# Counting TensorE's instruction records in the planner that orders an FNet + S4D kernel

## The chip, the cores and the metric

The kernel runs on one core of a Trainium2 chip. The core has a matrix engine (TensorE, in the profile PE, with its weight loads shown apart as PEld), a vector engine (VectorE, DVE), a scalar engine (ScalarE, ACT), GpSimd (POOL), and a queue engine (SyncE, SP) that issues nearly all transfers here. Each engine works through its own instructions in the order in which the program issued them, and waits on semaphores for the others.

The metric is the device time of one execution in microseconds, as the median of several runs. Before the change it is 602.95 us (three runs: 599.85, 602.95 and 603.13 us).

## What is computed

Two layers that share nothing but the output, whose halves are laid side by side:

```python
# A: FNet mixing of x[2048, 512]
a = einsum("sd,ed->se", x, dft_hid_re);  b = einsum("sd,ed->se", x, dft_hid_im)
y_a = einsum("ts,se->te", dft_seq_re, a) - einsum("ts,se->te", dft_seq_im, b)

# B: S4D convolution of u[2048, 512] with a kernel K of 512 x 2048, made from 128 modes
dt = exp(log_dt);  A = -exp(log_A_real) + 1j * A_imag;  C = (C_real + 1j * C_imag) * dt
P = exp((A * dt)[:, :, None] * arange(2048))
K = 2 * einsum("dn,dnl->dl", C, P).real
y_b = irfft(rfft(u, 4096) * rfft(K, 4096), 4096)[:2048] + u * D_skip

out = concatenate([y_a, y_b], axis=-1)
```

## The kernel before

**FNet** (class `Fnet`) is plain matrix work. Every fp32 operand is split into a rounded part `hi` and a rest `lo` (ScalarE copies at line 184, VectorE subtracts at line 188), and a product is three matmuls at line 304: hi·hi, hi·lo and lo·hi. There are 640 such steps of three matmuls, 128x128 by 128x512 each. An *item* is one streamed operand with four steps, one for each of four PSUM accumulators. Eight groups of 16 items make the sequence transform of x (results go out to DRAM as `p`), and four groups of 8 items multiply `p` with the hidden-dimension matrices. A split item lies in one of three pairs of buffers, a raw operand in one of four. Steps of FNet have the lowest priority (urgency 5): they are the filler between everything else.

**The S4D side** (class `Ssm`) is a chain. VectorE and ScalarE build tables `t1` and `t2` of the modes' powers for 16 chunks of 32 channels (`tables1`, `tables2`). For each chunk `taps` multiplies the tables on TensorE to get 32 channels of K. There is one `t2` buffer: `tables2` begins the next chunk's `t2` when the matmuls of `taps` have read the last one. Two chunks of K make one `stage1_k` (the first step of K's transform), whose result is stored as `xk`. `stage1_u` does the same for u, with u split in parts. For each of four quarters of the channels, four times, `product` takes the second step of both transforms (line 935), multiplies the spectra on VectorE, and takes a first inverse step (line 970), stored as `zs`. Two `inverse` calls per quarter (line 1015) end it and write `out_yb`. The last quarter of K is stored in four pieces (`store_k`), so that its products may begin one by one.

The S4D matmuls are small: a 32x32 or 64x32 tile against a few dozen to a few hundred columns. The change calls a group of them *dry*, because it uses up many instructions in little time. An fp32 matmul leaves two pairs of weight load and matmul records in the trace, so `taps` with its 64 matmuls is 256 records in about 2 us, where an FNet step of three matmuls is 6 records in about 0.7 us. If a first inverse step is waiting when `taps` is placed, the two are issued together (`other.run(got)`): 64 records at line 970 and then 256 at line 754. In the profile eight of the 16 `taps` are such joined groups.

**The order is planned, not written.** The program runs a small simulation (class `Plan`) while it emits instructions. Each piece of work is a Python generator that yields what it needs: an event, a buffer (`Sem`), or an engine with an estimated time, such as `yield "pe", 0.685` ahead of one FNet step or `yield "pe", 1.78 + (0.87 if other else 0)` ahead of `taps`. `run` keeps a list of pieces that ask for an engine and always takes the one with the smallest `key`: earliest possible start, then urgency, then age. Having taken it, it moves that engine's clock on by the estimate and resumes the generator, which issues its instructions then and there. So the order of `key` becomes the program order of every engine and of SP's queue. In the plan TensorE is only ever held up by data and buffers.

Of the kernel before, what the change touches and what calls it, by code (L numbers as in the profile page):

```python
# [48 lines left out]

HOP, RESULT, LATENCY = 0.3, 0.15, 3.3  # L50
STREAM = 5
APART = None, True


class Sem:


    def __init__(self, n):
        self.free, self.waiting = [0.0] * n, []
# [7 lines left out]
class Plan:  # L67
# [3 lines left out]
    def __init__(self):  # L71
        self.free, self.ready, self.now = {}, [], 0.0
        self.count, self.streaming = 0, True

    def spawn(self, gen, urgency=0, at=None):
        self.step([self.now if at is None else at, urgency, self.count, gen, None, None], None)
# [47 lines left out]

    def key(self, p):
        engine, _, *urgency = p[4]
        return max(p[0], self.free.get(engine, 0.0)), urgency[0]() if urgency and urgency[0] else p[1], p[2]

    def run(self):

        while self.ready:
            p = min(self.ready, key=self.key)
            engine, dur, *_ = p[4]
            start = self.key(p)[0]
            self.ready.remove(p)
            if engine == "pe":
                stream = p[1] >= STREAM
                if stream != self.streaming:
                    dur += 0.12 if stream else 0.1
                self.streaming = stream  # L140
            self.free[engine] = start + dur
            p[0] = start + dur + (LATENCY if engine.startswith("dma") else 0.0)
            self.step(p, start)
# [14 lines left out]
class Fnet:  # L158
# [38 lines left out]
    def warm(self):  # L197

        z, ps = self.pool.tile([128, DM], F32, name="y", bufs=STAGED), self.psum.tile([128, DM], F32, name="acc")
        yield "dve", 0.3  # L200
        self.nc.vector.memset(z, 0.0)
        yield "pe", 2.6
        for n in range(3):
            self.nc.tensor.matmul(ps[:, :256], z[:, :128], z[:, 256:], start=n == 0, stop=n == 2)

# [77 lines left out]
    def matmuls(self):  # L283
        nc = self.nc
        for g in self.groups:
            still = (self.x, self.x_ev) if g[0] == "s" else (self.w, self.w_ev)
            items, acc = self.items[g], []
            for batch in [[i] for i in items[:-BATCH]] + [items[-BATCH:]]:
                for d in range(4):
                    if batch[0][3] == 0:  # L290
                        yield self.acc
                        acc.append(self.psum.tile([128, DM], F32, name="acc"))
                    for i in batch:
                        k = i[3]
                        yield self.m_ev[i]
                        yield still[1][k] if k or d or g != self.groups[0] else self.x0_ev
                        (shi, slo), (mhi, mlo) = still[0][k], self.m[i]
                        yield "pe", 0.685
                        cols = slice(128 * d, 128 * d + 128)
                        three = (shi, mhi), (shi, mlo), (slo, mhi)  # L300
                        if still[1][k] is self.x_ev[0] and not d:
                            three = three[::2] + three[1:2]
                        for n, (l, r) in enumerate(three):
                            nc.tensor.matmul(acc[d], l[:, cols], r, start=k == 0 and n == 0,  # L304
                                             stop=k == len(items) - 1 and n == 2)
                        if d == 3:
                            self.plan.put(self.ss)
                            self.split_ahead -= 1
                            if i[:3] == ("s", 3, 1) and k < 8:
                                self.plan.set(self.x_free[k])  # L310
                    if batch[-1] is items[-1]:
                        self.plan.spawn(self.evacuate(g, d, acc[d]), -1)
# [53 lines left out]
class Ssm:  # L366
# [133 lines left out]
    def params(self, par, alpha, dt):  # L500

        v = self.nc.vector
        n = par.shape[2]
        yield "dve", dve(n), *APART
        v.tensor_tensor(par[:, 0], alpha, dt, op=OP.mult)
        yield "dve", dve(n), *APART
        v.scalar_tensor_tensor(par[:, 1], par[:, 1], 1.0 / (2 * math.pi), dt, op0=OP.mult, op1=OP.mult)
        yield "dve", dve(n), *APART
        v.tensor_tensor(par[:, 2], par[:, 2], dt, op=OP.mult)
        yield "dve", dve(n), *APART  # L510
        v.scalar_tensor_tensor(par[:, 3], par[:, 3], -1.0, dt, op0=OP.mult, op1=OP.mult)
# [224 lines left out]
    def taps(self, ks, n, done):  # L736

        nc = self.nc
        yield self.t1_ev[n]
        yield self.t2_ev[n]  # L740
        other = self.waiting.pop(0) if self.waiting else None
        got = yield from self.banks(2 if other else 1)
        k, p = got[0]
        yield "pe", 1.78 + (0.87 if other else 0)
        if other:
            other.run(got)
        t1, t2 = self.t1.pop(n), self.t2
        for o in range(2):
            ps = p[:, o, 256:].rearrange("p (i l) -> p i l", i=4)
            for i in range(4):  # L750
                for c in range(2):
                    for j in range(4):
                        d = 16 * o + 4 * i + j
                        nc.tensor.matmul(ps[32 * j:32 * j + 32, i], t1[:, d, c], t2[:, d, c],  # L754
                                         start=c == 0, stop=c == 1, tile_position=(0, 32 * j))
        self.plan.put(self.t1s)
        self.plan.put(self.t2s)
        self.taps_left -= 1
        if other:
            self.plan.set(other)  # L760
        while self.waiting and not self.taps_left:
            self.plan.set(self.waiting.pop(0))
        yield "act", act(512)
        nc.scalar.activation(ks[:, 8 * (n % 2):8 * (n % 2) + 8].rearrange("p (o i) l -> p o (i l)", o=2),
                             p[:, :, 256:], AF.Copy)
        if other:
            other.leave(k)
        else:
            self.give(k)
        done()  # L770

    def stage1_k(self, ks, n, ev):

        nc = self.nc
        yield ev
        yield "pool", 0.2
        nc.gpsimd.tensor_tensor(ks[:, :, 0], self.dskip[:, 16 * n:16 * n + 16], ks[:, :, 0], op=OP.add)
        yield self.const_ev
        got = yield from self.banks(2)
        yield "pe", 1.82  # L780
        for a in range(2):
            for j in range(4):
                r = slice(32 * j, 32 * j + 32)
                nc.tensor.matmul(got[j // 2][1][:, j % 2], self.f1k[r, a], ks[r, :, 32 * a:32 * a + 32],  # L784
                                 start=a == 0, stop=a == 1, tile_position=(32 * j, 0))
        self.plan.put(self.kss)
        yield self.xks
        xs = self.tab.tile([128, 32, 64], F32, name="xk_sb")
        for h, (k, p) in enumerate(got):
            for j in range(2):  # L790
                o = 32 * h + 16 * j
                yield from self.copy(xs[:, :, o:o + 16], p[:, j].rearrange("p (i l) -> p l i", i=16), n == 7 and j)
            self.give(k)
        xk = self.xk[n // 2].rearrange("s c l d -> (s c) l d")[:, :, 64 * (n % 2):64 * (n % 2) + 64]
        if n < 7:
            yield "dma", load(1024)
            for k in range(4):
                nc.sync.dma_start(xk[:, 8 * k:8 * k + 8], xs[:, 8 * k:8 * k + 8])
        else:
            for k in range(4):  # L800
                self.plan.spawn(self.store_k(xk, xs, k), 1)
            yield self.xk_ev[3][3]
        self.plan.put(self.xks)
        if n % 2 and n < 7:
            for ev in self.xk_ev[n // 2]:
                self.plan.set(ev)
        if n == 7:
            self.plan.set(self.tab_ev)
# [22 lines left out]
    def stage1_u(self, k, name):  # L831
        nc, b = self.nc, self.sets[0]
# [7 lines left out]
        yield "dve", dve(1024)  # L840
        nc.vector.tensor_tensor(lo, u, hi.bitcast(F32), op=OP.subtract)
        got = yield from self.banks(2)
        yield "pe", 1.42
        f_hi, f_lo = self.f1u_hi, self.f1u_lo
        for m in range(2):
            for n, (f, v) in enumerate(((f_hi, hi), (f_hi, lo), (f_lo, hi))):
# [6 lines left out]
        for m in range(2):  # L853
            n = 2 * k + m
# [69 lines left out]
    def product(self, b, h, q, got, done):  # L924
        nc, v, a = self.nc, self.nc.vector, self.nc.scalar
        uk = b.pool.tile([128, 2, 2, 2, 2, PART], F32, name="uk", bufs=b.n)
        yield "pe", 1.86
        xt = self.xt[h, q]
        for r in range(2):
            for c in range(2):  # L930
# [44 lines left out]
            yield w  # L975
        if w.got is None:
            got = yield from self.banks(2)
            yield "pe", 0.95
            w.run(got, False)
        self.plan.put(b.uks)  # L980
        yield b.zbs
# [22 lines left out]
    def inverse(self, b, h, i, n):  # L1004
# [4 lines left out]
        for o in range(0, n, 8):  # L1009
            nc.sync.dma_start(z[:, o:o + 8], self.zs[h].rearrange("s c l d -> (s c) l d")[:, n * i + o:n * i + o + 8])  # L1010
        (k, ps), = yield from self.banks(1)
        yield "pe", 0.1 + 0.1025 * n
        for w in range(n // 2):
            for y in range(2):
                nc.tensor.matmul(ps[64 * y:64 * y + 64, w // 4, PART * (w % 4):PART * (w % 4) + PART],  # L1015
# [87 lines left out]
```

## Time and profile before

| | us |
|---|---|
| median of the three runs | 602.95 |
| the profiled execution's own time | 596.78 |
| its span, first to last instruction | 595.0 |
| TensorE (PE) busy | 579.2 |
| VectorE (DVE) busy | 508.1 |
| ScalarE (ACT) busy | 387.1 |

The profiled execution is 6.2 us shorter than the median of the runs and 3.1 us shorter than the shortest of them. It ran at a granted TensorE clock of 0.999. A busy share is an average over the whole span; what matters is which wait ends last at each place. By fortieths of the span, VectorE is 80% busy or more in all slices but one from the second until about 490 us, where the tables are done, and far less busy in the rest. TensorE is 80% busy or more in all slices but the last.

### The profile page before, as it was taken

How to read it: one execution, taken by the hardware profiler on the slowest of the kernel's cores; microseconds unless marked ns; L12 is line 12 of the kernel's file. 1: busy time of each engine (PE TensorE's matmuls, PEld its weight loads, DVE VectorE, ACT ScalarE, POOL GpSimd, SP SyncE). 2: the span in 40 equal slices, each digit the busy share in tenths (PEclk: the TensorE clock that was granted, in tenths of full speed). 3: DMA queues.
4: the chain of work that ended last, by engine and by line, in shares of the span. 5: the costliest groups of instructions: out<-in, count | busy, mean ns of one | idle time of the engine just before them, and what ended most of it. 6: DMA issues, size and time to landing. Idle time of an engine off the chain costs nothing.

```text
span 595.0 us, 14993 instructions
## 1 busy us (share of the span) xinstructions
PE 579.2 (97%) x5990; PEld 442.6 (74%) x5990; DVE 508.1 (85%) x898; ACT 387.1 (65%) x748; POOL 4.8 (1%) x12
## 2 busy tenths in 40 slices
PE   8999999999999999999998989998999999989997
PEld 6877777778778777777876768776877777766786
DVE  7999999999999999999998969998999993265420
ACT  5789877976785777749683858594866454353432
POOL 0000000000000000000000000000000000000000
PEclk9999999999999999999999999999999999999999
DMA  8977847665483376636877485557697946997474
GB/s 278 385 259 263 286 153 278 234 218 192 124 271 96 102 202 200 163 106 190 222 230 230 156 217 153 140 165 216 223 292 216 293 139 189 269 335 238 139 255 143
DMA packets 141238, 125.84 MB, mean 211 GB/s; under 512 B 46192, under 2 KB 106352, under 8 KB 140912
## 3 DMA queue, kind: packets, MB, share of 16 engines
q1 hardware_dynamic: 140880, 124.48, 67.5%
q8 instruction: 47, 0.77, 0.5%
q10 hardware_dynamic: 288, 0.39, 0.2%
q14 instruction: 23, 0.19, 0.1%
HBM read 82.12 MB, written 42.73 MB: 210 GB/s over the span
## 4 chain that ended last, share of the span: by engine, by line
PE 85%; DVE 4%; ACT 3%; DMA 3%; issue 3%; SPq 1%; DVEq 0%; ACTq 0%
PE acc L304 65%; PE f L754 5%; PE f L935 4%; PE f L970 3%; PE f L784 3%; PE f L1015 2%; PE f L849 2%; DVE lo L188 1%; DMA p<-y 1%; DMA out_yb<-zl 1%; ACT hi L184 1%; DMA xt<-xk 1%; DMA cs<-in_ldt 1%; ACT y L327 1%; DVE x_lo L188 1%
## 5 line engine op out<-in xcount | busy, mean ns | idle before, releaser
L304 PE MATMUL acc<-hi,x_hi 128*128 128x512 f32 x640 | 258.1, 403 | 1.7 <-ACT y L327 1.5
L304 PE MATMUL acc<-lo,x_hi 128*128 128x512 f32 x640 | 250.3, 391 | 0.3 <-DVE lo L188 0.3
L304 PE MATMUL acc<-hi,x_lo 128*128 128x512 f32 x640 | 249.8, 390 | 0.0
L558 DVE TENSOR_TENSOR prod<-t,cs 128x1024 f32<-128x1024 f32 (+3 forms) x192 | 164.1, 870 | 9.9 <-ACT t L696 8.1
L304 PEld LDWEIGHTS acc<-hi,x_hi 128*128 128x128 f32 x640 | 120.2, 188 | 49.3 <-issue 19.8
L184 ACT ACTIVATE hi<-raw 128x512 fp32r<-128x512 f32 x160 | 100.5, 629 | 77.1 <-PE acc L304 61.0
L188 DVE TENSOR_TENSOR lo<-raw,hi 128x512 fp32r<-128x512 f32 x160 | 109.4, 686 | 41.1 <-ACT hi L184 39.7
L304 PEld LDWEIGHTS acc<-hi,x_lo 128*128 128x128 f32 x640 | 120.3, 188 | 26.4 <-DVE x_lo L188 0.3
L304 PEld LDWEIGHTS acc<-lo,x_hi 128*128 128x128 f32 x640 | 120.5, 188 | 23.9 <-DVE lo L188 1.2
L567 DVE TENSOR_TENSOR t<-prod 128x512 f32<-128x512 f32 (+4 forms) x192 | 94.4, 511 | 1.2
L574 ACT ACTIVATE square<-t 128x256 f32<-128x256 f32 (+1 forms) x64 | 36.6, 571 | 22.9 <-DVE t L567 22.7
L327 ACT ACTIVATE y<-acc 128x512 f32<-128x512 f32 x47 | 27.9, 595 | 17.1 <-PE acc L304 14.4
L754 PEld LDWEIGHTS f<-t,t 128*32 128x32 f32 x2048 | 29.7, 110 | 12.3 <-issue 7.7
L754 PE MATMUL f<-t,t 128*32 128x64 f32 x2048 | 32.7, 220 | 5.9 <-issue 5.4
L947 ACT ACTIVATE uk<-f 128x1024 f32<-128x1024 f32 x32 | 31.9, 1013 | 9.8 <-PE f L935 6.4
L935 PE MATMUL f<-xt,w 64*32 64x256 f32 x1024 | 31.5, 379 | 2.7 <-DMA xt<-xk 2.0
L950 DVE TENSOR_TENSOR z<-uk 128x512 f32<-128x512 f32 x32 | 21.9, 686 | 13.4 <-ACT uk L947 13.4
L935 PEld LDWEIGHTS f<-xt,w 64*32 64x32 f32 x1024 | 18.6, 106 | 13.7 <-issue 7.4
L439 ACT ACTIVATE z<-f 128x512 f32<-128x512 f32 x28 | 15.7, 597 | 18.2 <-PE f L970 10.1
L587 DVE TENSOR_TENSOR t<-square 128x128 f32<-128x128 f32 (+1 forms) x64 | 24.7, 385 | 0.0
L633 ACT ACTIVATE cs<-cs 128x352 f32<-128x352 f32 x32 | 15.9, 540 | 11.8 <-DVE cs L628 11.7
L581 DVE SCALAR_TENSOR_TENSOR t<-t 128x128 f32<-128x128 f32 (+2 forms) x48 | 22.3, 465 | 0.3
(89 smaller groups left out, 433.7 us busy)
## 6 DMA issues: line engine op xcount, KB each, us to landing
raw<-in_sT SPq DMA_DIRECT2D x127, 256.0 KB, 3.2
p<-y SPq DMA_DIRECT2D x32, 256.0 KB, 3.4
xk<-xk_sb SPq DMA_DIRECT2D x32, 256.0 KB, 4.0
xt<-xu SPq DMA_DIRECT2D x32, 256.0 KB, 3.9
xt<-xk SPq DMA_DIRECT2D x32, 256.0 KB, 5.0
zs<-z SPq DMA_DIRECT2D x32, 256.0 KB, 3.0
zl<-zs SPq DMA_DIRECT2D x16, 512.0 KB, 6.5
raw<-p SPq DMA_DIRECT2D x32, 256.0 KB, 3.4
```

What stands on the lines that cost most here:

```text
L184: self.nc.scalar.activation(hi, src, AF.Copy)
L188: self.nc.vector.tensor_tensor(lo, src, hi.bitcast(F32), op=OP.subtract)
L304: nc.tensor.matmul(acc[d], l[:, cols], r, start=k == 0 and n == 0, stop=k == len(items) - 1 and n == 2)
L327: self.nc.scalar.activation(y, ps, AF.Copy, scale=-1.0 if g[2] == 1 else 1.0)
L558: self.nc.vector.tensor_tensor(p.rearrange("p k d c m -> p k (d c) m"), src.rearrange("p d c l -> p (d c) l")[:, None, :, rows].to_broadca ...
L567: self.nc.vector.tensor_tensor(dst[:, :, :, rows], p[:, 0], p[:, 1, :, ::-1], op=OP.add)
L574: self.nc.scalar.activation(sq, t[:, :, :, m // 2:m], AF.Square)
L581: self.nc.vector.scalar_tensor_tensor(t[:, :, 1, m:2 * m:2], t[:, :, 0, m // 2:m], 2.0, t[:, :, 1, m // 2:m], op0=OP.mult, op1=OP.mult)
L587: self.nc.vector.tensor_tensor(t[:, :, 0, m:2 * m:2], box[0][:, :, 0], box[0][:, :, 1], op=OP.subtract)
L754: nc.tensor.matmul(ps[32 * j:32 * j + 32, i], t1[:, d, c], t2[:, d, c], start=c == 0, stop=c == 1, tile_position=(0, 32 * j))
L935: nc.tensor.matmul(both[:, :, c], self.w2[rows, 2 * q + r, xx, 32 * c:32 * c + 32], xt[rows, r, xx], start=True, stop=True, tile_position= ...
L947: a.activation(uk[:, r].rearrange("p g n c d -> p g (n c d)"), p, AF.Copy)
```

## The change

No arithmetic, buffer or transfer is added or removed. What changes is how `Plan` computes the start of a piece of work on TensorE, and so which of two pieces it takes.

- Each request for TensorE now carries the number of records that it will issue: 12 for the warm-up, 6 for an FNet step, 257 for `taps` alone, 322 for `taps` with a waiting inverse step, 33 for `stage1_k`, 25 for `stage1_u`, 130 for `product`, 65 for an inverse step alone, and `4 * n + 1` (65) for `inverse`.
- `Plan` counts the records issued (`done`) and keeps a list of instruction blocks of 256 records with the time at which each arrives. In its model, block k is asked for 3.0 us after record 256k + 129 and no sooner than 4.3 us after the one before, arrives 2.4 us after it was asked for, and is needed at record 256k + 449.
- `fetched` works out, for a request of n records, how long it would be held by a block that has not arrived, within the request or within as many records behind it. `key` adds this to the start.

A request with such a hold therefore counts as starting later, and any FNet step that is ready before then is taken first. In the diff `r[3]` is the number of records and `r[1]` the estimated time.

```diff
+BLOCK, ASKS, LASTS = 256, 129, 449
+ASKED, APART_BY, COMES = 3.0, 4.3, 2.4
...
         self.count, self.streaming = 0, True
+        self.done, self.blocks, self.asked = 0, [], -9.0
...
     def key(self, p):
         engine, _, *urgency = p[4]
-        return max(p[0], self.free.get(engine, 0.0)), urgency[0]() if urgency and urgency[0] else p[1], p[2]
+        start = max(p[0], self.free.get(engine, 0.0))
+        if engine == "pe":
+            start += self.fetched(p[4], start)[0]
+        return start, urgency[0]() if urgency and urgency[0] else p[1], p[2]
+
+    def fetched(self, r, start):
+
+
+        n, dur = r[3], r[1]
+        wait, blocks, asked = 0.0, list(self.blocks), self.asked
+        while BLOCK * len(blocks) + ASKS < self.done + n:
+            at = start + wait + dur * max(0, BLOCK * len(blocks) + ASKS - self.done) / n
+            asked = max(at + ASKED, asked + APART_BY)
+            blocks.append(asked + COMES)
+        for k, b in enumerate(blocks):
+            run = BLOCK * k + LASTS - self.done
+            if 0 <= run < n:
+                wait += max(0.0, b - (start + wait + dur * run / n))
+            elif 0 <= run < 2 * n:
+                wait += max(0.0, b - (start + wait + dur + 0.11 * (run - n)))
+        return wait, blocks, asked
...
             if engine == "pe":
+                _, self.blocks, self.asked = self.fetched(p[4], max(p[0], self.free.get(engine, 0.0)))
+                self.done += p[4][3]
...
-        yield "pe", 2.6
+        yield "pe", 2.6, None, 12
...
-                        yield "pe", 0.685
+                        yield "pe", 0.685, None, 6
...
-        yield "pe", 1.78 + (0.87 if other else 0)
+        yield "pe", 1.78 + (0.87 if other else 0), None, 322 if other else 257
...
-        yield "pe", 1.82
+        yield "pe", 1.82, None, 33
...
-        yield "pe", 1.42
+        yield "pe", 1.42, None, 25
...
-        yield "pe", 1.86
+        yield "pe", 1.86, None, 130
...
-            yield "pe", 0.95
+            yield "pe", 0.95, None, 65
...
-        yield "pe", 0.1 + 0.1025 * n
+        yield "pe", 0.1 + 0.1025 * n, None, 4 * n + 1
```

## The prediction

> **What bounds the kernel now.** I read the page first: the busy shares, the queues, and the costliest groups.
>
> ```profile
> span 595.0 us, 14993 instructions
> PE 579.2 (97%) x5990; PEld 442.6 (74%) x5990; DVE 508.1 (85%) x898; ACT 387.1 (65%) x748; POOL 4.8 (1%) x12
> q8 instruction: 47, 0.77, 0.5%
> PE 85%; DVE 4%; ACT 3%; DMA 3%; issue 3%; SPq 1%; DVEq 0%; ACTq 0%
> ```
>
> TensorE is busy for 579.2 of 595.0 us, so it is idle for 15.8 us, and no reordering can save more than that. It leaves 5990 + 5990 = 11980 records, and queue q8 brought 47 instruction packets of 0.77 MB together, 16 KB each: 255 records to a packet. So q8 carries TensorE's program, a packet for each 256 records. Next the waits of TensorE, then the chain of waits where it says "issue", and its end:
>
> ```profile
> PE f L754 <- issue: 5.4, 3, 2.1
> PE f L935 <- DMA xt<-xk: 2.0, 1, 2.0
> PE acc L304 <- ACT y L327: 1.5, 2, 0.9
> PE acc L304 <- DVE lo L188: 0.3, 1, 0.3
> ```
> ```profile
> 314.43 1.63 issue
> ...
> 349.83 2.09 issue
> ...
> 406.81 1.67 issue
> ...
> 580.27 1.90 PE f L1015 x32
> 582.17 9.08 PE acc L304 x39
> ```
>
> Columns of the chain are start, length, and what. A third of TensorE's idle time, 1.63 + 2.09 + 1.67 = 5.39 us, lies in three holes at line 754 (`taps`), in which no semaphore is waited for. The steps of FNet (line 304) wait only 1.8 us in all of 1920 matmuls: their operands are nearly always there. The chain ends in 9.08 us of FNet matmuls with nothing else, so the end is set by how much TensorE work is left, not by the S4D chain.
>
> Are the three holes the holds that the change models? The timeline of TensorE around them, with the windows that end inside each hole and those that end where its group begins (the counts after PE and PEld are records):
>
> ```profile
> 312.45 1.97 PE L754 MATMUL f<-t,t 128*32 128x64 f32 x123
> 316.05 0.31 PE L754 MATMUL f<-t,t 128*32 128x64 f32 x5 [1.63 <-issue]
> 351.91 0.24 PE L754 MATMUL f<-t,t 128*32 128x64 f32 x1 [2.09 <-issue]
> 408.48 0.42 PE L754 MATMUL f<-t,t 128*32 128x64 f32 x13 [1.67 <-issue]
> ```
> ```profile
> 0.00:315.00 315.00, 311.07 (x3024) 240.68 (x3025) 305.88 (x555) 233.00 (x464) 2.65 (x8) 1.00 0.67 212
> 0.00:351.00 351.00, 344.84 (x3405) 266.23 (x3405) 338.42 (x609) 256.45 (x510) 2.89 (x9) 1.00 0.67 211
> 0.00:407.50 407.50, 399.62 (x4040) 307.95 (x4041) 391.54 (x705) 295.38 (x587) 3.55 (x10) 1.00 0.66 206
> 0.00:311.40 311.40, 308.04 (x2869) 238.27 (x2869) 302.39 (x549) 231.98 (x462) 2.65 (x8) 1.00 0.66 212
> 0.00:346.80 346.80, 341.81 (x3248) 263.82 (x3248) 335.67 (x606) 255.21 (x508) 2.89 (x9) 1.00 0.67 211
> 0.00:403.90 403.90, 396.71 (x3893) 305.65 (x3893) 388.01 (x701) 294.35 (x585) 3.55 (x10) 1.00 0.66 205
> ```
>
> The holes come after 6049, 6810 and 8081 records: 761 and 1271 apart, against 3 x 256 = 768 and 5 x 256 = 1280, which leaves 7 and 9 for semaphore records that this count lacks. All three cut a joined group of 320 matmul and load records, after 311, 314 and 295 of them. And q8's packet stands just ahead of the end of each hole; its rows for 313.3 to 313.6, 349.5 to 349.8 and 405.8 to 406.1 us:
>
> ```profile
> q8 instruction: 1, 0.02, 22.2%
> ```
> ```profile
> q8 instruction: 1, 0.02, 19.2%
> ```
> ```profile
> q8 instruction: 1, 0.02, 21.2%
> ```
>
> TensorE resumes 2.1 to 2.8 us after a time in these windows. It runs out of program there: the mechanism is real. [...]
>
> **The change, part by part.** *Which holds does the plan foresee?* In the diff's model a block is needed 449 - 129 = 320 records after the one that asks for it, and comes 3.0 + 2.4 = 5.4 us after it. A group runs into a hold if those 320 records take less. Asking records stand 320 - 311 = 9, 320 - 314 = 6 and 320 - 295 = 25 records ahead of the three groups. The pace of FNet's six records:
>
> ```profile
> 309.95 0.39 PE L304 MATMUL acc<-hi,x_hi 128*128 128x512 f32 x1
> ...
> 310.63 0.39 PE L304 MATMUL acc<-hi,x_hi 128*128 128x512 f32 x1
> ```
>
> One step starts 0.68 us after the one before, 0.113 us a record. A joined group is planned at 1.78 + 0.87 = 2.65 us for 322 records, 0.0082 us each. First: 9 x 0.113 + 311 x 0.0082 = 3.6 us, a hold of 1.8. Second: 0.7 + 2.6 = 3.3, a hold of 2.1. Third: 2.8 + 2.4 = 5.2, a hold of 0.2 in the model, where the chip took 1.67 because the block came late. A `taps` alone (257 records) would have its asking record at least 63 records ahead, 7.1 us, so it is foreseen to run free; smaller groups too. The code also looks past a group for a hold in the FNet steps behind it; the waits above show none of those on the chip.
>
> *What is saved.* FNet steps are put ahead until the hold is gone: each moves the group by 0.685 us and takes up 6 records, 0.05 us, so 1.8 / 0.635 takes three and 2.1 / 0.635 takes four. TensorE does these steps in time that it now sits idle, and they are missing later from the 9.08 us at the end: 1.63 + 2.09 = 3.72 us. The third hold I count as unchanged: 0.2 us foreseen would bring one step, 0.64 us of 1.67; bounds 0 and 1.67, and I take 0, since the asking record shifts by some records either way when steps move.
>
> *What it costs on TensorE.* The work is the same and so is the number of changes between FNet and small groups: FNet, group, FNet stays, with three or four steps on the other side. No row shows a cost for the step moved; I take 0.
>
> *What is behind the held group.* `taps` now ends at the time at which the hold let it end, plus what the steps overshoot: 3 x 0.68 - 1.63 = 0.4 and 4 x 0.68 - 2.09 = 0.6 us. Behind it waits the copy into the one `t2` buffer (line 696), and then VectorE:
>
> ```profile
> 318.22 0.41 DVE L558 TENSOR_TENSOR prod<-t,cs 128x128 f32<-128x128 f32 x1 [1.53 <-ACT t L696]
> ```
> ```profile
> 354.01 0.85 DVE L558 TENSOR_TENSOR prod<-t,cs 128x128 f32<-128x128 f32 x2 [4.42 <-ACT t L696]
> ```
> ```profile
> 410.77 0.41 DVE L558 TENSOR_TENSOR prod<-t,cs 128x128 f32<-128x128 f32 x1 [1.91 <-ACT t L696]
> ```
>
> So VectorE pays for each held group too, 7.9 us in all, and this the change does *not* give back: the steps go ahead of the group, they don't make its program come sooner. The tables and the last K come some 1.0 us later. What covers that is the end: the last `out_yb` is issued by 579.85 + 3.87 = 583.7 and lands 3.4 us later (median), at 587.1, 7.9 us ahead of the span's end.
>
> ```profile
> 579.85 3.87 SPq L1024 DMA_DIRECT2D out_yb<-zl  x2
> ```
> ```profile
> out_yb<-zl SPq DMA_DIRECT2D x2, 512.0 KB, 3.4
> ```
>
> With 3.72 us of FNet gone from the end and K 1.0 us later, 3.2 us of that cushion are left. If it were gone, what K is late by would be added to the end.
>
> *What moves with the steps.* A step that ends an item frees a `raw` buffer, so one load of FNet (SP, line 272) per item is issued up to 2.7 us earlier in SP's order, and three or four steps are one item. SP works in order, and this is what it pays there over the whole run:
>
> ```profile
> SPq L272 <- DVE lo L188: 122.0, 72, 4.5
> ```
>
> A mean of 1.7 and at most 4.5 us for a raw load that waits for VectorE, with `xt`, `zs` or `xk` transfers queued behind it. Around the first two holes this delays loads that no row shows TensorE waiting for: 0. In the last quarter TensorE does wait for `xt<-xk` (2.0 us above), and that place moves with the plan. If TensorE arrives there 3.72 us sooner and the load doesn't, all is given back; if the new order fills the wait, 2.0 us more are won. I take 0, since the plan has FNet steps to put there; both ends are kept.
>
> **Sum.** 3.72 us off the profiled execution: 595.0 to 591.3 in span, 596.78 to 593.1 in its own time. The median of the runs shown, 602.95, is 6.17 us above that execution, which no row explains; taking the saving from the median gives 602.95 - 3.72 = 599.2 us.
>
> **The rivals.** (1) *All three holds go*, because records shift so that the third is foreseen: 5.39 us, 597.6. For it: the model is 0.2 us from acting there. Against: the block came late, and the model's constants don't know that.
> (2) *The gain is given back*: the wait for `xt<-xk` grows by the 3.72 us, or shifted records let a late block catch another group for 1.6 to 2.1 us a time: about 602.9. For it: VectorE gets nothing, and the third hold shows that the model can miss. Against: the FNet work at the end.
> (3) *The plan does not do on the chip what it says*: its clock differs from the chip's, no FNet step is ready there in the plan, and the holes stay: 603.0. [...] Against: the counts above, which fit within 1%.
> (4) *Slower*, by SP's queue in the last quarter. FNet being further on puts raw loads ahead of the `xk` pieces and `xt` loads; each may hold the queue for 4.5 us while TensorE stands at line 935 in its fixed order. One such wait gives 4.5 - 3.7 = 0.8 us back net; two make it 9.0 - 3.7 = 5.3 us slower, 608.3; it decides against the change from 3.72 us on. For it: the wait of 2.0 us is there now. Against: the plan sees the queue.
>
> **How the numbers follow.** Chances: two holds go 0.42; all three 0.20; given back 0.18; nothing happens 0.10; SP's queue 0.10. The likeliest gives 599.2 (597.2 to 601.2, with 2.0 us either way for the wait at line 935). The range goes from 595.5, which is 597.6 less that wait, to 603.5, which holds the second and third rivals with half a microsecond, and leaves out the slower case. About 1% is what a measurement of this kernel can tell, 6 us: faster than 596.9 takes all three holds and part of the wait, or two and all of it with some luck: 0.08 + 0.08 = 0.16. Slower than 609.0 is the far part of the last rival and mishaps of a new order: 0.07. Within 1%: 0.77.
>
> **What would show it.** In the changed profile, the wait of line 754 for "issue" should fall from 5.4 to about 1.7 us, with three or four more FNet steps ahead of the groups near 313 and 349 us; VectorE's waits for the copy at line 696 should not fall; the FNet matmuls behind the last `inverse` should shrink from 9.08 to about 5 us. I am wrong if holes in other groups take their place, if the wait at line 935 grows past 5 us, or if the last `out_yb` lands at the very end.

## The result, and the profile after

| | before | changed |
|---|---|---|
| median of 14 runs, us | 599.56 | 595.32 |
| lowest and highest, us | 595.66, 603.13 | 592.72, 597.54 |
| profiled execution, own time and span, us | 596.78, 595.0 | 597.54, 595.8 |

The ratio is 0.9929, with a 95% interval of 0.9904 to 0.9954. The kernel became 0.7% faster, where 0.6% was forecast; but the time, 595.32 us, lies 0.2 us below the range, because the 602.95 us from which the saving was taken was itself 3.4 us above the median of 14 runs. Of the changed kernel the profiled execution is the slowest of the 14; that of the kernel before was faster than 13 of its 14. So the two spans hardly differ and must be read stage by stage.

First TensorE's waits in the changed kernel (us in total, times, longest); line 779 is `taps`, 754 before, and 329 is FNet's step, 304 before:

```profile
PE f L779 <- issue: 3.5, 1, 3.5
PE f L960 <- DMA xt<-xk: 2.2, 1, 2.2
```

One hold is left instead of three, and it is longer than any before. The chain of waits of the changed kernel shows what became of each:

```profile
307.01 8.40 PE acc L329 x36
315.42 1.05 PE f L995 x32
316.46 2.19 PE f L779 x128
...
343.68 1.05 PE f L995 x32
344.73 1.92 PE f L779 x128
...
401.15 1.85 PE f L779 x121
403.00 3.50 issue
406.50 0.32 PE f L779 x7
406.82 4.54 PE acc L329 x12
...
580.36 1.90 PE f L1040 x32
582.25 9.76 PE acc L329 x42
```

And the stretch of FNet ahead of the first held group in the kernel before:

```profile
305.11 6.37 PE acc L304 x27
```

The first group has 36 instead of 27 FNet matmuls in front, three steps more, and is not held; its 128 matmuls take 0.3 us longer than those of the second (2.19 against 1.92). The second, near 344 us, runs in 1.92 us. In the third the program runs out after 121 of 128 matmuls, for 3.50 us. And that is not all it costs: the 12 FNet matmuls behind it take 4.54 us, where 12 take 2.95 us elsewhere. Windows of the changed kernel (the third figure from the right is the granted TensorE clock):

```profile
398.00:403.00 5.00, 5.00 (x163) 3.81 (x162) 4.93 (x7) 2.32 (x5) 0.00 (x0) 1.00 0.99 328
403.00:406.50 3.50, 0.00 (x0) 0.00 (x0) 1.41 (x2) 0.00 (x0) 0.00 (x0) 1.00 0.57 203
406.50:410.00 3.50, 3.50 (x15) 2.76 (x15) 0.99 (x2) 2.75 (x8) 0.00 (x0) 0.55 0.31 86
```

After the idle 3.5 us the clock is granted at 0.55 for 3.5 us, which costs 0.45 x 3.5 = 1.6 us more. A second profile of the same kernel (run e4 below) has the same hold at 2.4 us, a granted clock of 1.00 in the 3.5 us behind it, and a span of 590.3 us:

```profile
PE f L779 <- issue: 2.4, 1, 2.4
```

### The profile page after: what moved, and what is told of

Same layout as the page of the kernel before. It is cut to its first block, busy times and chain, and to the rows that moved or that the text cites. A ratio compares the mean times of both kernels' runs of the same rounds, so it can differ in the third digit from the quotient of the medians.

```text
span 595.8 us, 14996 instructions
## 1 busy us (share of the span) xinstructions
PE 581.8 (98%) x5990; PEld 445.3 (75%) x5990; DVE 507.9 (85%) x898; ACT 387.0 (65%) x748; POOL 5.1 (1%) x12
## 4 chain that ended last, share of the span: by engine, by line
PE 95%; DMA 2%; ACT 2%; issue 1%; SPq 0%; DVE 0%; ACTq 0%
PE acc L329 74%; PE f L779 5%; PE f L960 5%; PE f L995 3%; PE f L809 3%; PE f L1040 3%; PE f L874 2%; DMA xt<-xk 1%; DMA uk<-in_x 1%; ACT hi L209 0%; ACT seed L628 0%; ACT y L352 0%; ACT x_hi L209 0%; ACT uk L864 0%; SPq L933 0%
## 5 line engine op out<-in xcount | busy, mean ns | idle before, releaser
L213 DVE TENSOR_TENSOR lo<-raw,hi 128x512 fp32r<-128x512 f32 x160 | 109.5, 686 | 50.9 <-ACT hi L209 50.5
```

The lines of the kernel that those rows point to most:

```text
L213: self.nc.vector.tensor_tensor(lo, src, hi.bitcast(F32), op=OP.subtract)
```

## Experiments

Two theories were put against each other. *Holds*: the time goes with the length of the holds at `taps`, where the program comes late, and with nothing else of the change. *Order*: the gain comes from the new order as such, in which the S4D chain runs some 5 us earlier and VectorE no longer waits. Each run below was timed beside runs of the kernel before on the same chip; holds are the stops behind record 256k + 449 in its one profile (k counts the blocks of 256 records from 0).

| run | holds, us | median, us | ratio to before (95%) |
|---|---|---|---|
| e1 before, again | 5.2 | 598.66 | 0.996 (0.994 to 0.999) |
| e5 64 records added behind the holds | 5.2 | 597.44 | 0.998 (0.995 to 1.000) |
| e10 first hold left out of the key | 2.7 | 596.30 | 0.996 (0.994 to 0.998) |
| e4 changed kernel, again | 2.4 | 595.73 | 0.993 (0.990 to 0.995) |
| e3 32 records added at the start | 1.9 | 593.53 | 0.988 (0.985 to 0.992) |
| e2 64 records added at the start | 0 | 591.08 | 0.984 (0.980 to 0.987) |
| e9 first hold alone in the key | 0.4 | 590.90 | 0.989 (0.985 to 0.993) |
| e8 longer margin, 20 records | 0 | 590.49 | 0.987 (0.985 to 0.989) |
| e6 64 records at no added time | 0 | 590.26 | 0.986 (0.984 to 0.988) |
| e7 longer margin alone | 1.4 | 620.83 | 1.036 (1.032 to 1.041) |

The kernel before, run as a copy of itself (e1), came out at 0.996 with an interval that leaves out 1, so differences of 0.4% are not told apart here.

### Both kernels again (e1, e4)

No edit. The first is the kernel before, the second the changed one.

> The kernel before, unchanged, for a second profile of it. If the holds theory is right (TensorE runs out of program when a block of 256 records comes late against record 256k + 449), the second profile has its holds at the same three records, 6081, 6849 and 8129, and no others in joined groups, with 1.5 to 4 us each; a hold of over 3 us shows a lower granted clock behind it. If the holds were accidents of transfers (rival), they would lie at other records.

> The changed kernel again, for a second profile. Holds theory: one hold, at record 8129 near 403 us, of 1 us (as the block model has it) to 3.5 us (as in the first profile), and the granted clock falls below 1 behind it only where it lasts over 3 us. Ratio as measured, 0.993. Rival: the remaining hold was an accident of the first profile and is gone.

Waits of TensorE in e1:

```profile
PE f L754 <- issue: 5.2, 3, 1.8
```

Counted in the start times of the trace, the program ran out after exactly the expected records: 6081, 6849 and 8129 = 256k + 449 for k = 22, 25 and 30, in both profiles of the kernel before; and after 8129 in both of the changed one. These are no accidents of single transfers. The limit of 3 us in both expectations was the author's estimate and is not shown: of the holds only the 3.50 us of the changed kernel was longer, with 0.55 behind it, and in e1 the clock fell to 0.52 behind a wait of 2.4 us (last section).

### The boundaries moved, the order kept (e2, e3, e5, e6)

Small matmuls are added to the warm-up of the kernel before. The plan isn't told, so every engine's order stays as it was, but each block of 256 records ends earlier in the work. For e2:

```diff
         for n in range(3):
             self.nc.tensor.matmul(ps[:, :256], z[:, :128], z[:, 256:], start=n == 0, stop=n == 2)
+        for n in range(16):
+            self.nc.tensor.matmul(ps[:32, :16], z[:, :32], z[:, 256:272], start=True, stop=True)
```

> The kernel before, in its own order, with 16 small matmuls (64 records) added to the warm-up, whose product is overwritten. Nothing else moves, but every block boundary falls 64 records earlier in the work. Holds theory: by the block model no group is held any more, so 5.4 us of holds go, less at most 1 us for the added matmuls: ratio 0.990 to 0.994, and no wait of line 754 for issue over 0.5 us unless a block comes over 1.5 us late. Rival (the gain of the change comes from its new order, the S4D chain being 5 us earlier): the order is that of before, so the ratio is 1.00.

TensorE's waits in e2, all of them:

```profile
PE f L937 <- DMA xt<-xk: 1.8, 1, 1.8
PE acc L204 <- DVE y L201: 1.6, 1, 1.6
PE acc L306 <- ACT y L329: 1.5, 2, 0.9
PE f L756 <- ACT uk L949: 0.5, 1, 0.5
```

No wait for issue is left, and the kernel takes 591.08 us, ratio 0.984 (0.980 to 0.987): about twice the gain of the change, in the order of before. The order theory gave 1.00 and falls: the new order isn't needed for the gain. Whether it adds anything of its own in the changed kernel no run shows. The gain is larger than was expected (0.990 to 0.994). Between the two profiles it is 595.0 - 589.5 = 5.5 us, of which 5.4 less the 1.8 us that the added matmuls take make 3.6; shorter waits make another 1.2 (1.8 instead of 2.7 us at line 935, and none for `lo`). The medians differ by 9.6 us; the clock, told below, is likely a part of the rest (0.999 or more in five of the six runs of e2, in 3 of the 21 of the kernel before beside them), and what it leaves stays open.

The control e5 issues the same 16 matmuls ahead of the ninth FNet group, behind the three held groups:

```diff
                         yield "pe", 0.685
+                        if g == ("p", 0, None) and k == 0 and d == 0:
+                            w0 = shi.bitcast(F32)
+                            for n in range(16):
+                                nc.tensor.matmul(acc[d][:32, :16], w0[:, :32], w0[:, :16], start=True, stop=True)
```

> Control for the 64 added records: the kernel before with the same 16 small matmuls, but issued ahead of the ninth group of FNet (near 467 us), behind the three held groups; their product is overwritten. Holds theory: the three holds stay at records 6081, 6849 and 8129, 5 to 6 us in all, and the time is that of before plus at most 2 us: ratio 1.000 to 1.003. Rival (the added matmuls help for another reason, such as the clock at the start or a later start): ratio near that of the early ones, 0.984, or at least well below 1.

```profile
PE f L758 <- issue: 5.2, 3, 1.9
```

The three holds are there, at the same records, and the ratio of 0.998 (0.995 to 1.000), a little below the 1.000 expected, is not told apart from that of the kernel against itself. So it is where the records stand that helps, not the added matmuls.

e3 is e2 with `range(8)`:

> The same with 8 small matmuls (32 records). Holds theory: the three old holds go and two new ones come, at the joined group near 259 us (about 2.7 us) and at taps near 494 us (about 1.3 us), so the ratio lies between that of 64 records and 1: about 0.996. Rival (order): 1.00, with no hold at 259 us.

```profile
PE f L756 <- issue: 1.9, 2, 1.3
```

The time lies in between, as expected, though nearer to e2 (0.988 instead of 0.996) and not for the reason given. No hold came near 259 or 494 us; two of the old ones were left, shorter, at records 6849 and 8129. The block model has the right records, but its times are off: in e3 the packets start from 2.0 us ahead of the model's time to 6.0 us behind it. Worked out from the start times in the trace, block 30 is by the model asked for by record 7809, and its packet starts 5.7, 5.6, 5.9 and 4.3 us later in the first four profiles of the two kernels, where the model has 3.0; for block 17 it is 1.5 us in the first profile. Over 282 blocks in six profiles this delay is 2.2 us in the median when the DMA engines were under half busy meanwhile (57 blocks), and 3.5 us when they were busier (225 blocks). That loaded engines delay the packet is thus likely; no run tested it, and why block 30 is late in these profiles stays open.

e6 keeps 76 records in the warm-up but only one of the three large matmuls:

```diff
-        for n in range(3):
-            self.nc.tensor.matmul(ps[:, :256], z[:, :128], z[:, 256:], start=n == 0, stop=n == 2)
+        self.nc.tensor.matmul(ps[:, :256], z[:, :128], z[:, 256:], start=True, stop=True)
+        for n in range(18):
+            self.nc.tensor.matmul(ps[:32, :16], z[:, :32], z[:, 256:272], start=True, stop=True)
```

> The early 64 records at no added time: the warm-up's three large matmuls become one large and 18 small ones, 76 records instead of 12; the rest is the kernel before in its order. Holds theory: no hold, and FNet starts 1.5 us earlier than with 16 added matmuls (1.89 us there): ratio 0.981 to 0.983. Rival (a long warm-up is what helped): 0.99 or more.

There was no hold, and the ratio is 0.986 (0.984 to 0.988): no better than e2 beyond the uncertainty. A long warm-up isn't what helped. The 1.5 us at the start were not won; in its profile FNet's first steps wait there for the split of x instead.

### One foreseen hold at a time (e9, e10)

In the changed kernel only block 22, the first hold, enters the key (e9), or all blocks but this (e10, with `==`):

```diff
         for k, b in enumerate(blocks):
+            if k != 22:
+                continue
             run = BLOCK * k + LASTS - self.done
```

> The changed kernel, with only block 22 (the first hold) entering the key. Three FNet steps go ahead of the group near 311 us; what follows is ordered anew because that group is later in the plan. Theory: the first hold goes by the steps put ahead, the second goes because the group behind it now starts 30 records further from its block's asking record, not because steps were put ahead there; the third is not foreseen and, with its group beginning 20 records before the asking record, the program runs out just behind the group, at record 8129, for 2 to 4 us if block 30 is late again. Ratio about that of the change, 0.990 to 0.996. Rival (each foreseen hold saves its own length and nothing else moves): the second hold stays, 2 us, and the ratio is 0.997.

The chain of waits of e9 around the third group:

```profile
393.81 1.05 PE f L997 x32
394.86 1.92 PE f L781 x128
396.78 2.74 PE acc L331 x11
399.52 0.39 issue
399.91 2.56 PE acc L331 x10
```

Three steps put ahead of one group are nearly the whole benefit: no hold at 6081, none at 6849, and 0.4 us at 8129 behind the group, in the middle of an FNet step. (I had expected 2 to 4 us there, if block 30 was late again. Its packet came 3.8 us behind record 7809, not 4.3 to 5.9 as in the two kernels, and FNet's steps behind the group use up the last records slowly; no run parts the two.) The second hold thus goes without a step being put ahead there. The first group comes 2 us later in the plan, `stage1_k` and an `inverse` behind it change places, and the second group then begins 30 records earlier in the count, so that its block is needed only behind it, where FNet uses up records slowly (0.113 us each). By its median, 590.9 us, e9 is ahead of the whole change at 595.3 and 595.7, though the intervals of the ratios overlap. (TensorE also waits 3.6 us at line 962 in e9, at records 10605 and 10779, which end no block: the products of the last quarter, as in the other kernels.)

> The changed kernel with block 22 left out of the key and all others in. Theory: the first hold stays at record 6081 (1.6 to 2.1 us), four FNet steps more stand ahead of the group near 347 us and its hold at record 6849 goes, and the third group begins 34 records behind the asking record, which covers a block on time and leaves about 1 us of a late one. Two holds and 2.5 to 3.5 us in all, ratio 0.992 to 0.997. Rival (steps put ahead only move the hold): a hold of about 2 us stays at record 6849.

Waits in e10, and its windows between 401 and 408 us:

```profile
PE acc L331 <- ACT y L354: 3.9, 3, 2.3
PE f L781 <- issue: 2.7, 2, 1.6
```
```profile
401.40:403.80 2.40, 0.10 (x1) 0.00 (x0) 2.40 (x5) 2.36 (x6) 0.00 (x0) 1.00 1.01 317
...
404.10:407.60 3.50, 3.50 (x9) 2.33 (x8) 3.50 (x6) 0.63 (x1) 0.00 (x0) 0.51 0.91 295
```

The first hold stays at 1.6 us. At the second, the steps put ahead take the hold from 2.09 to 1.1 us and not to 0, again because its block came later than the model has it (the packet 5.0 us behind its record instead of 3.0). The third is gone, but in this order FNet stops at nearly the same place, 2.3 us for ScalarE's copy of an accumulator, and the slow clock follows. Two holds with 2.5 to 3.5 us together were expected, and 2.7 us are measured, but that the sum fits is luck: the second was to go and the third to stay.

### A margin for late blocks (e7, e8)

```diff
-ASKED, APART_BY, COMES = 3.0, 4.3, 2.4
+ASKED, APART_BY, COMES = 3.0, 4.3, 5.0
```

> The changed kernel with one constant changed: a block comes 5.0 us after it was asked for instead of 2.4, which covers the 2.6 us by which block 30 came late. Holds theory alone: no holds, so a ratio near 0.984. Rival (fourth of the prediction, in another place: steps put ahead hold back the S4D chain, and FNet runs out before the chain ends): the S4D chain ends far behind the last FNet step, TensorE waits at the end, and the time is 20 to 36 us longer than before: ratio 1.03 to 1.06. The program's own order speaks for the rival, since it has no FNet step behind the third product of the last quarter.

TensorE's longest waits in e7, and the end of its chain:

```profile
PE f L1040 <- DMA zl<-zs: 8.3, 1, 8.3
PE f L960 <- issue: 7.0, 1, 7.0
```
```profile
598.60 0.70 DVE z L975
599.32 0.70 DVE uk L977
600.05 0.70 DVE uk L985
600.88 2.45 PE f L995 x32
603.36 0.70 DVE z L461
604.52 2.81 DMA zs<-z
607.34 4.12 DMA zl<-zs
611.59 5.49 PE f L1040 x64
```

The holds are gone but for one of 1.4 us (the 7.0 us above end at record 11288, which ends no block), and the kernel is 3.6% slower. With so long a hold foreseen, FNet steps were put ahead of so many groups that the S4D chain ended last: nothing of FNet is left behind 564 us, and VectorE, DMA and the last matmuls follow one another with TensorE idle between. In this end the clock was granted at 0.50 for 23.9 us from 574.3 us on and for 13.6 us from 601.6 us on, so a part of the 22 us lost is the slow clock behind the waits and not the chain's order alone; no run parts the two. So this is what makes the change dangerous: the steps put ahead are borrowed from the end, and the cushion there is the 7.9 us of the prediction.

e8 has the same constant and 20 records more in the warm-up (`range(5)` as in e2, and the plan told 32 instead of 12):

> The same constant with 20 records of small matmuls added to the warm-up and counted by the plan. The order comes out otherwise, with 24 FNet steps left for the last two inverses and the end. Holds theory: no hold of over 0.5 us anywhere: 0.984. Rival (chain too late): only two FNet steps follow the last inverse, so whatever the chain is late by adds to the end: 0.99 to 1.00.

No wait for issue is left, and the time is 590.49 us, 0.987 (0.985 to 0.989), close to the holds theory; the chain's lateness cost nothing that can be told. Twenty records at the start decide between 620.8 and 590.5 us with the same planner.

## Why the prediction was right, and where it failed

**The bound and the mechanism** were right. The three holes are the program running out at 256k + 449 records (e1, e2, e5), and TensorE's idle time sets the end: in the table, e7 apart, the time falls with the holds, from about 598 us at 5.2 us of holds to about 590.5 us at none.

**The step that failed is the base of the sum**: "taking the saving from the median gives 602.95 - 3.72 = 599.2". The profile's execution stood 6.17 us below that median, "which no row explains", and I took the median of three runs as if it were settled. From the median of 14, the same saving gives 599.56 - 3.72 = 595.84, against 595.32 measured; as a ratio, 0.9938 against 0.9929 (0.9904 to 0.9954). So 3.39 of the 3.88 us by which the forecast missed are the base.

What no row explained is in part the clock. The profiled execution had a granted clock of 0.999. Of the 21 runs of the kernel before that stood beside e1 to e4, only 3 had 0.999 or more (median 598.1 us); 9 had 0.996 to 0.997 (600.0 us) and 9 had 0.993 to 0.994 (600.9 us). A stretch of 3.4 us at half clock, as the changed kernel has from 406.88 to 410.29 us, takes 0.5 x 3.4 / 595 = 0.003 off the mean, so by this estimate these are runs with one or two such stretches, at 1.7 us each. That explains 2 to 3 of the 6.17 us; the rest stays open. Nor is the split the same everywhere: beside e5 to e8, 7 of 17 runs of the kernel before had 0.999 or more, and in e10 the five runs at 0.999 or more were no faster than the six at 0.996 or 0.997 (596.5 and 596.2 us). Of the 18 runs without a hold in their kernel's profile (e2, e6, e8), 17 had 0.998 or more. Of the 48 runs of e1, e4, e5 and the changed kernel itself, with 2.4 us of holds or more, 10 had. So long holds and a lower clock come together; but of 17 holds in the profiles only one, the 3.50 us of the changed kernel, had half clock right behind it, and what brings the slow stretches in the other runs is not shown.

**The two holds that go** came out as forecast in number, for one of two reasons. At the first, three steps stand ahead, as worked out (360 FNet steps precede the group instead of 357). At the second I forecast four steps more; there are five fewer (387 instead of 392), and the hold went because of the new order behind the first (e9). That it went was luck. Where four steps are indeed put ahead (396 in e10), about half the hold is left.

**The third hold** I took as unchanged at 1.67 us, "since the asking record shifts by some records either way". This term failed too. The group begins at record 7822 instead of 7834, so 13 records instead of 25 lie between its block's asking record, 7809, and the group: at 0.113 us a record, 1.4 us less until the program is used up. The hold was foreseen but not filled: in the plan that the changed kernel makes as it is built, it counts 1.07 us, and the next FNet step is ready only 1.44 us after the group. So the hold grew, to 3.50 and 2.4 us in the two profiles, the first with 1.6 us of slow clock behind it. Two holds of 3.72 us went and this one gave back 0.7 to 3.4 us of them in the profiles, which leaves 0.3 to 3.0 us. That the medians differ by 4.24 us, near the 3.72 of the sum, is thus in part luck. From the first profile of the kernel before to that of e4 the span falls by 4.7 us: 3.0 by the holds, 1.0 by shorter waits (0.5 us at line 935, 0.5 us at line 754 for `uk`), and 0.7 us that is not accounted for.

**VectorE** I forecast to get nothing back. Its waits for the copy into `t2`, of the kernel before and then of the changed one, were:

```profile
DVE prod L558 <- ACT t L696: 8.1, 4, 4.4
```
```profile
DVE prod L583 <- ACT t L721: 0.2, 1, 0.2
```

In the new order VectorE has other work while `t2` is being read: from 300 to 360 us, around the first two groups, it is busy for 59.3 us instead of 53.4. But over the whole span it is as busy as before (507.9 against 508.1 us), and its waits for ScalarE's `hi` grew from 39.7 to 50.5 us. My forecast was wrong there, and it had no price: by the chains, the last `stage1_k` begins 3.4 us earlier (495.06 against 498.46), and still the end is set by what is left of TensorE's work.

**The end** has not the 5 us of FNet that I forecast but 9.76: the saved time stands ahead of the whole last quarter, not behind it. In e4's profile the last `inverse` begins at 574.92 us, against 580.27 before, with the same 9.76 us behind it; in the first profile of the changed kernel, where the third hold and the clock behind it took 3.4 us more than before, it begins at 580.36. The wait for `xt<-xk` stayed (2.2 after 2.0), as I took it. The fourth rival, in which the S4D chain is held back until it ends last, didn't happen in the changed kernel; e7 shows it in another place, the chain as a whole instead of SP's queue, 22.0 us above the kernel before (620.83 against 598.84 us beside it).

## What to carry to other kernels

Where many small matmuls meet, count TensorE's records: idle time without a semaphore that recurs at the same record modulo 256 (here 193, as in 6081, 6849 and 8129) was here the program coming late, and moving the boundary by 64 padding records in the warm-up (ratio 0.984 to 0.986) was cheaper and safer than re-planning the order. The number has to be tried: 32 records left two holds (e3). In a greedy plan one decision reorders all that follows, so a foreseen saving should be tested one decision at a time. And take the base of a forecast from enough runs to know its spread, beside the granted clock of the one that was profiled.

## What the runs showed of the hardware

Stops shorter than the 3.50 us of the changed kernel can be followed by half clock. In e10 TensorE stood still for 2.33 us, and from 404.1 us on the clock was granted at 0.51 for 3.5 us (windows above). In e1 a wait of 2.4 us for `xt<-xk` ended at 527.6 us, and these windows follow:

```profile
525.00:527.50 2.50, 0.22 (x1) 0.00 (x0) 0.78 (x2) 0.18 (x1) 0.00 (x0) 1.00 1.13 286
...
528.80:532.30 3.50, 3.50 (x37) 2.19 (x21) 1.39 (x2) 1.48 (x2) 0.00 (x0) 0.52 0.92 296
```

In e4 a hold of 2.4 us was followed by full clock:

```profile
404.50:408.00 3.50, 3.50 (x52) 2.52 (x58) 2.11 (x6) 2.47 (x8) 0.00 (x0) 1.00 0.48 132
```

So of these three stops of 2.3 to 2.4 us two were followed by half clock and one was not. The slow stretch lasted 3.4 to 3.5 us in these profiles (0.51 to 0.55 in windows of 3.5 us), and far longer in e7: 23.9 us at 0.50, which set in during a stop of 7.0 us at line 960 and outlasted two more of 0.7 us.

All 17 holds in nine profiles come after record 256k + 449. That record 256k + 129 asks for the block is the model's; what the traces show is that no packet started before it, and none sooner than 1.0 us behind it, in any of the twelve profiles. In the four profiles of the two kernels the packets start 1.1 to 8.9 us behind that record. A group of small matmuls that is safe by the model's 3.0 us may still be held, as the second in e10 was, for 1.1 us with its packet 5.0 us behind the record.
